# A fused convolution and feed-forward kernel: sums scaled in the first statistics pass, a longer warm-up, a last row cut 320 to 192, and a new order of all instructions

## The chip, the cores and the metric

The kernel runs on one core of a Trainium2 chip. The metric is the time of one execution on the device in microseconds (us); lower is better. A core has five engines that run side by side: TensorE (PE, matmuls and transposes), VectorE (DVE), ScalarE (ACT), GpSimd (POOL) and SyncE (SP), which here only issues transfers. PEld in the profile is TensorE's loading of the stationary operand. Matmuls write to PSUM, eight banks of 128 partitions by 2 KB; everything else lives in SBUF.

## What the reference computes

One sequence of S = 2048 rows with D = 512 columns passes through two pairs of layers, A, B, A, B, all in bfloat16 with the same weights in both pairs.

```
A(q):  k_shift = causal 4-tap convolution of k along the sequence, one set of taps per column
       kv      = k_shift * v
       y       = causal convolution of kv with ssm_k (2048 taps per column, by FFT) + kv * ssm_D
       A(q)    = q * y
B(x):  (silu(x @ w_gate) * (x @ w_up)) @ w_down,   F = 1792

x = A_q
x = x + A(layernorm(x)); x = x + B(layernorm(x))
x = x + A(layernorm(x)); x = x + B(layernorm(x))
```

The layer norm has no weights: (x - mean) / sqrt(var + 1e-5) over the 512 columns. k, v and ssm_k are the same in both A layers, so y is computed once.

## The kernel before

**Tiling.** The sequence is cut into NB = 4 blocks of 512 rows; a block is held as 128 partitions by R = 4 rows. y is made block by block with a short Fourier transform that is a set of matmuls: `fwd` holds cosine and sine tables, `inv` their transposes; H, X and Z are spectra of ssm_k, of kv and of their products. The feed-forward layer takes half a block at a time: a *unit* is (layer, block c, half h) with two rows per partition, and there are 16 of them. For each of 14 tiles `ft` of F a unit makes 4 matmuls of 256 columns for gate and 4 for up (line 968, reported as L311 since the helper `mm` issues them) into a PSUM tile `pf`, ScalarE takes silu of the gate (L970, `sg`) and copies the up part (L974, `ht`), VectorE multiplies them (L977), and the product is the stationary operand of the down matmuls of 512 columns (L990, into `pd`). ScalarE copies `pd` to `dn` (L1034) and VectorE adds it to the block of x, named `xc` (L1037).

**Layer norm.** `prologue` normalises a half block, multiplies it with y, adds it to x, normalises again to `z`, and transposes z into `zT`, the moving operand of gate and up: by transposing transfers on SP (L893), and in the very first unit by TensorE (L920, `ptz`) with one copy each on VectorE and ScalarE (L923, L925). Statistics come from VectorE (`ln_stats`: bnst, mv, ve) or, for eight of the half blocks, from ScalarE (`ln_stats_act`). The latter makes a pass over each of two rows that sums them (L828), one small instruction that multiplies the sums by -1/512 to `nm` (L831), a pass each that squares the row plus nm and sums that (L834), and `ve` (L838). GpSimd raises ve to the power -1/2 (`rstd`).

**Order.** The program does not issue instructions where they are written. Each call of `plan.add` records an instruction with its engine and its buffers; the table `ORDER` gives each of the 1568 its place, and `Plan.issue` emits them by it. Each engine then runs its own instructions in that order and waits by semaphores for the data and the buffers that an instruction needs. Buffers come from rings of a fixed size: `pf` has 4 PSUM tiles, `pc` and `pd` 2 each, `zT` 3, `z` 3, `ht` 5.

**Start.** SP issues the loads of hn (ssm_k of block 0), kn (k), vt (v), xc (q), then those of block 1 and the weight wg, the two table transposes `inv`, and then wu and wd, wd in two parts. VectorE and ScalarE make the tables. TensorE turns the taps (`pt4`, L1133), then transposes hn (16 matmuls, L477) and kn (16, L366). VectorE, ScalarE and GpSimd make 16 diagonal matrices `dg` of the taps (L1152, L1148). Where the planner's own times leave TensorE idle for over 0.5 us before 32 us, `issue` puts in warm-up matmuls `wm` on a constant tile `wz`: their number is the gap, less 0.3 us on both sides at the very start and 0.3 us elsewhere, over 0.106 us.

**End.** The last unit's second row is computed as two halves of 256 columns in two PSUM tiles. x of the second half is added in PSUM by a matmul with the identity (L949). VectorE adds the first half to x (L1008), ScalarE copies the second (L1011), and SP and ScalarE each issue one output transfer (L1014).

Of the kernel before, what the change touches and what calls it, by code (L numbers as in the profile page):

```python
# [9 lines left out]
P = 128  # L10
# [8 lines left out]
NB = 4  # L19
# [31 lines left out]
LASTV = True  # L51
ORDER = [
# [58 lines left out]
]  # L111
R = 4

NS = 8
# [122 lines left out]
def kernel(  # L239
# [984 lines left out]
    def run(unit):  # L1224
        ffn(unit)
# [75 lines left out]
```

## Time and profile before

| | |
|---|---|
| median of 3 runs | 344.79 us (344.21 to 345.18) |
| profiled execution, own time | 344.93 us |
| its span | 343.20 us |
| busy: TensorE, VectorE, ScalarE, GpSimd | 336.4, 283.4, 253.9, 35.3 us |
| first gate matmul, end of the last down matmul | 33.58, 339.98 us |
| waiting transfers at the start: hn of block 0, its issue and first use | 0.72, 4.34 us |

Busy time of TensorE counts every matmul from its start to its modelled end; these overlap, so a busy TensorE may still be far from its full rate. The number behind a line, such as L311, is the line in the kernel, or in the helper that issued the instruction. In a list of events each row has the start, the length, the engine, the line, the tiles written and read, and how many instructions were merged; a bracket gives the engine's idle time just before and what ended it.

### The profile page before, as it was taken

Reading aid. Unit: us, or ns where it says so; the run is one execution under the profiler, and the core shown is the slowest. Engines: PE = TensorE matmul, PEld = TensorE weight load, DVE = VectorE, ACT = ScalarE, POOL = GpSimd, SP = SyncE. Lnnn points to the kernel's source line nnn. Section 1 sums busy time; section 2 is a strip of 40 time slices with the busy share of each in tenths; the row PEclk is TensorE's granted clock in tenths of the full one; section 3 lists DMA queues with packets and bytes.
Section 4 is the critical chain, followed back from the end, with each engine's and each line's share of the span. In section 5 each row is a group of like instructions: output and inputs, shape, how many; then the busy total and the mean of one; then the engine's idle time right before and its main releaser. Section 6 shows DMA issues by size and latency. Waiting matters only on the chain.

```text
span 343.2 us, 6553 instructions
## 1 busy us (share of the span) xinstructions
PE 336.4 (98%) x2579; PEld 248.6 (72%) x2610; DVE 283.4 (83%) x482; ACT 253.9 (74%) x504; POOL 35.3 (10%) x46
## 2 busy tenths in 40 slices
PE   8999999999999999999999999999999999999996
PEld 7756868768687676858586777768685877777783
DVE  8899999899999999899999999989998433726022
ACT  6999999899997765958789995779475464446261
POOL 4010100203111000103110100201101001000000
PEclk9999999999999999999999999999999999999999
DMA  7999218310116044040101014210101100110101
GB/s 273 336 316 341 52 27 112 77 32 0 34 31 94 14 95 138 2 94 3 32 2 46 2 46 79 76 32 1 32 0 33 35 13 0 39 39 8 24 26 37
DMA packets 42088, 22.95 MB, mean 67 GB/s; under 512 B 33861, under 2 KB 39882, under 8 KB 42058
## 3 DMA queue, kind: packets, MB, share of 16 engines
q1 hardware_dynamic: 41904, 22.47, 26.6%
q8 instruction: 20, 0.33, 0.4%
q14 instruction: 10, 0.08, 0.1%
q10 hardware_dynamic: 154, 0.07, 0.1%
HBM read 12.33 MB, written 2.10 MB: 42 GB/s over the span
## 4 chain that ended last, share of the span: by engine, by line
PE 91%; ACT 4%; DVE 3%; issue 1%
PE pf L311 54%; PE pd L990 28%; PE ps L311 6%; PE ps L458 1%; ACT H L419 1%; PE wm L1267 1%; DVE bnst L809 1%; ACT hs L487 1%; PE pt L477 1%; ACT X L419 0%; ACT n L859 0%; PE pt L366 0%; DVE m L540 0%; DVE t L665 0%; DVE Z L667 0%
## 5 line engine op out<-in xcount | busy, mean ns | idle before, releaser
L311 PE MATMUL pf<-zT,wu_sb 128*128 128x256 bf16 x896 | 110.4, 273 | 0.1
L311 PE MATMUL pf<-zT,wg_sb 128*128 128x256 bf16 x896 | 110.2, 273 | 0.2
L990 PE MATMUL pd<-wd_sb,ht 128*128 128x512 bf16 (+1 forms) x440 | 102.4, 372 | 1.2
L311 PEld LDWEIGHTS <-wu_sb 128*128 128x128 bf16 x896 | 87.7, 98 | 16.4
L311 PEld LDWEIGHTS <-wg_sb 128*128 128x128 bf16 x896 | 87.6, 98 | 16.5 <-issue 0.8
L974 ACT CAST ht<-pf 128x512 bf16<-128x512 f32 x112 | 64.0, 591 | 29.3 <-PE pf L311 29.1
L970 ACT ACTIVATE sg<-pf 128x512 bf16<-128x512 f32 x112 | 65.5, 603 | 17.4 <-PE pf L311 15.1
L990 PEld LDWEIGHTS <-ht 128*128 128x128 bf16 x462 | 45.2, 98 | 42.5
L977 DVE TENSOR_TENSOR ht<-ht,sg 128x1024 bf16<-128x1024 bf16 (+1 forms) x64 | 39.0, 617 | 24.0 <-ACT sg L970 18.7
L814 POOL TENSOR_TENSOR rstd<-ve,nhalf 128x2 f32<-128x2 f32 x24 | 23.0, 958 | 217.8 <-DVE ve L812 207.6
L1034 ACT CAST dn<-pd 128x512 bf16<-128x512 f32 x30 | 17.0, 589 | 21.0 <-PE pd L990 20.9
L809 DVE BATCH_NORM_STATS2 bnst<-xc 128x6 f32<-128x512 bf16 x48 | 31.6, 684 | 0.6
L419 ACT ACTIVATE X<-ps 128x512 bf16<-128x512 f32 x32 | 19.2, 611 | 4.0 <-PE ps L311 3.4
L653 DVE TENSOR_TENSOR t<-X,G 128x2048 bf16<-128x2048 bf16 x18 | 21.9, 1218 | 0.1
L657 DVE TENSOR_TENSOR t<-X,G 128x2048 bf16<-128x2048 bf16 x18 | 21.9, 1216 | 0.0
L1037 DVE TENSOR_TENSOR xc<-xc,dn 128x1024 bf16<-128x1024 bf16 x15 | 10.3, 689 | 13.4 <-ACT dn L1034 13.2
L665 DVE TENSOR_TENSOR t<-t,t 128x2048 bf16<-128x2048 bf16 x12 | 14.7, 1222 | 0.3
L667 DVE TENSOR_TENSOR Z<-Z,t 128x2048 bf16<-128x2048 bf16 x12 | 14.6, 1220 | 0.2
L840 POOL TENSOR_TENSOR rstd<-ve,nhalf 128x2 f32<-128x2 f32 x8 | 8.7, 1088 | 59.2 <-ACT ve L838 59.1
L419 ACT ACTIVATE H<-ps 128x512 bf16<-128x512 f32 x24 | 13.8, 610 | 0.1
L886 DVE TENSOR_TENSOR n<-n,Yk 128x1024 bf16<-128x1024 bf16 x15 | 10.3, 688 | 4.1 <-ACT n L859 3.8
L604 ACT ACTIVATE kc<-kTb,tapF 128x512 bf16<-128x512 bf16 x16 | 12.1, 783 | 0.0
(105 smaller groups left out, 323.3 us busy)
## 6 DMA issues: line engine op xcount, KB each, us to landing
hn<-in_A_ssm_k_dram SPq DMA_DIRECT2D x4, 512.0 KB, 4.1
vt<-in_A_v_dram SPq DMA_DIRECT2D x4, 512.0 KB, 5.9
xc<-in_A_q_dram SPq DMA_DIRECT2D x4, 512.0 KB, 5.3
out_dram<-xc SPq DMA_DIRECT2D x15, 128.0 KB, 1.8
wg_sb<-in_B_w_gate_dram SPq DMA_DIRECT2D x1, 1792.0 KB
wu_sb<-in_B_w_up_dram SPq DMA_DIRECT2D x1, 1792.0 KB, 8.5
wd_sb<-in_B_w_down_dram SPq DMA_DIRECT2D x1, 1280.0 KB, 12.0
kn<-in_A_k_dram SPq DMA_DIRECT2D x1, 512.0 KB, 4.5
```

What stands on the lines that cost most here:

```text
L311: nc.tensor.matmul(o, lhsT=lhsT, rhs=rhs, start=(n == 0), stop=(n == len(terms) - 1))
L419: add("ACT", act(D), lambda: nc.scalar.activation(out=view(), in_=ps.t[:], func=ACT.Copy, scale=scale), r=[ps], w=[(buf, keys)], conv=conv)
L653: dve(n * D, lambda t1=t1, part=part: nc.vector.tensor_mul(out=t1.t[:], in0=x.t[:, sl, 0, :], in1=g.t[:, sl, part, :]), [(x, key(slots, (0 ...
L657: dve(n * D, lambda t2=t2, part=part: nc.vector.tensor_mul(out=t2.t[:], in0=x.t[:, sl, 1, :], in1=g.t[:, sl, 1 - part, :]), [(x, key(slots ...
L665: dve(n * D, lambda t1=t1, t2=t2, comb=comb: nc.vector.tensor_tensor(out=t1.t[:], in0=t1.t[:], in1=t2.t[:], op=comb), [t2], [t1], conv=conv)
L809: add("DVE", 0.6, lambda st=st, i=i: nc.vector.bn_stats(out=st.t[:], in_=xs[c].t[:, i, :]), r=[(xs[c], (i,))], w=[st])
L814: add("POOL", pw, lambda: nc.gpsimd.tensor_tensor(out=rstd.t[:], in0=ve.t[:], in1=nhalf.t[:].to_broadcast((P, n)), op=ALU.pow), r=[ve, nha ...
L970: add("ACT", act(D), lambda ps=ps, o=o, sg=sg: nc.scalar.activation(out=sg.t[:, o:o + 2, :], in_=ps.t[:], func=ACT.Silu), r=[ps], w=[(sg, ...
L974: add("ACT", act(D), lambda ps=ps, o=o, ht=ht: nc.scalar.copy(out=ht.t[:, o:o + 2, :], in_=ps.t[:]), r=[ps], w=[(ht, (o // 2,))], due=(uni ...
L977: dve(n * W, lambda sg=sg, ht=ht: nc.vector.tensor_mul(out=ht.t[:], in0=ht.t[:], in1=sg.t[:]), [sg], [ht], due=(unit, k / pairs, 0.0, "h"))
L990: nc.tensor.matmul((pds[o] if not cs.start else pds[HP]).t[:, cs], lhsT=ht.t[:, q, o * P:(o + 1) * P], rhs=wt["d"].t[:, ft, cs], start=(ft ...
L1034: add("ACT", act(D), lambda o=o: nc.scalar.copy(out=dn.t[:, o, :], in_=pds[o].t[:]), r=[pds[o]], w=[(dn, (o,))], due=(unit, 1.0, 3.0, "h"))
```

## The change

- `ln_stats_act` gives its summing pass the scale -1/512, so that the sum is minus the mean, and uses it as nm; the small instruction L831 is gone. The squaring pass of a row depends on that row's sum alone.
- The warm-up's operand is a constant tile of ones that the framework writes, read with step 0; `wz` and its memset are gone. The number of warm-up matmuls leaves out the margins: the gap less 0.3 us at the very start, the whole gap where TensorE falls idle before 8 us, the gap less 0.3 us later.
- The last row is cut into 320 and 192 columns.
- The three `zT` tiles are slices of one tile `zall`.
- The feed-forward code is split into `gate_up` and `down`, which could share a group of tiles between two units. `SHARE` is empty, so each unit makes the same groups of 4, 4, 4 and 2 as before. `VE_D` is off, so `ve` stays on ScalarE.
- The prologue of unit (1, c, 0) is written ahead of unit (0, c, 1); the instructions are the same.
- `ORDER` is a new table with 1559 places, nine fewer: eight times nm and the memset of wz.

In the new order, by comparing the two tables: the transposes of hn run in the order of rows 3, 2, 1, 0 instead of 0, 2, 1, 3 in time, and all 16 transposes of kn come ahead of the first matmul on hs (8 before); VectorE makes six diagonals and two negated tables between tapF and its first copy of hs (four and two before); one matmul group of X1 instead of two, and no statistics pass on ScalarE, precedes the first gate matmul; two evacuations of H come ahead of the first normalisation on ScalarE; on SP the first part of wd is issued behind hn and vt of block 2; on POOL the memset of kTb comes behind three diagonals.

```diff
+TAIL = 320
+VE_D = False
+SHARE = {}
 ORDER = [
-    0, 8, 122, 2, 4, 5, 12, 9, 3, 6, 1, 31, 32, 33, 10, 14, 7, 11, 15, 16, 18, 21, 17, 20, 22, 23, 36, 30, 56, 73, 153, 24, 40, 25, 41, 34, 42, 38,
...
+    0, 14, 2, 4, 6, 8, 21, 1, 3, 5, 12, 13, 63, 9, 10, 11, 7, 16, 22, 19, 17, 18, 20, 23, 30, 43, 31, 73, 88, 89, 29, 44, 25, 36, 26, 45, 24, 33, 55,
...
 ]
+NZ = 3
@@
-                            n = int((start - max(t, 0.3) - 0.3) / 0.106)
+                            n = int((start - t - (0.0 if 0.0 < t < 8.0 else 0.3)) / 0.106)
@@
+        if ring == "zT":
+            def cut(slot):
+                if zall.t is None:
+                    zall.t = zall.make(0)
+                return zall.t[:, slot]
+            return plan.buf(ring, name, cut, parts)
...
+    zall = whole("zT", [P, NZ, KD, HP, P])
@@
-                    out=jk.t[:], in_=xs[c].t[:, i, :], func=ACT.Copy, accum_out=sm.t[:, o:o + 1]), r=[(xs[c], (i,))], w=[jk, (sm, (o,))], after=after)
-        nm = new("mv", "nm", [P, n], F32)
-        add("ACT", TINY, lambda: nc.scalar.mul(out=nm.t[:], in_=sm.t[:, 0:n], mul=-1.0 / D), r=[(sm, range(n))], w=[nm])
+                    out=jk.t[:], in_=xs[c].t[:, i, :], func=ACT.Copy, scale=-1.0 / D, accum_out=sm.t[:, o:o + 1]), r=[(xs[c], (i,))], w=[jk, (sm, (o,))], after=after)
+        nm = sm
...
-                r=[(xs[c], (i,)), nm], w=[jk, (sm, (n + o,))])
+                r=[(xs[c], (i,)), (nm, (o,))], w=[jk, (sm, (n + o,))])
@@
+            halves = (slice(0, TAIL), slice(TAIL, D))
...
-            for half_, (eng, cs) in enumerate((("DVE", slice(0, D // 2)), ("ACT", slice(D // 2, D)))):
+            for half_, (eng, cs) in enumerate((("DVE", slice(0, TAIL)), ("ACT", slice(TAIL, D)))):
@@
-    wz = whole("wz", [P, P])
-    add("DVE", 0.07, lambda: nc.vector.memset(wz.t[:], 0.5), w=[wz], due=-80)
+    ones = nc.const_aps.tensor(1.0, (P, P), BF16)
@@
         run((0, c, 0))
+        prologue(1, c, 0)
         run((0, c, 1))
-        prologue(1, c, 0)
         prologue(1, c, 1)
@@
-            nc.tensor.matmul(t[:], lhsT=wz.t[:], rhs=wz.t[:], start=True, stop=True)
+            nc.tensor.matmul(t[:], lhsT=ones, rhs=ones, start=True, stop=True)
```

More of the change, by code (lines that the diff above doesn't have):

```diff
@@ L231, in issue @@
                 if b.t is None:
-                    b.t = b.make(place.get(b, 0))
+                    b.slot = place.get(b, 0)
+                    b.t = b.make(b.slot)
                 if b in place:
@@ L835, in ln_stats_act @@
                 out=jk.t[:], in_=xs[c].t[:, i, :], func=ACT.Square, bias=nm.t[:, o:o + 1], accum_out=sm.t[:, n + o:n + o + 1]),
-                r=[(xs[c], (i,)), nm], w=[jk, (sm, (n + o,))])
+                r=[(xs[c], (i,)), (nm, (o,))], w=[jk, (sm, (n + o,))])
         ve, rstd = new("ve", "ve", [P, n], F32), new("rs", "rstd", [P, n], F32)
-        add("ACT", TINY, lambda: nc.scalar.activation(out=ve.t[:], in_=sm.t[:, n:2 * n], func=ACT.Identity, scale=1.0 / D, bias=eps.t[:]),
-            r=[(sm, range(n, 2 * n)), eps], w=[ve])
+        if VE_D:
+            add("DVE", 0.08, lambda: nc.vector.tensor_scalar(out=ve.t[:], in0=sm.t[:, n:2 * n], scalar1=1.0 / D, scalar2=LN_EPS,
+                                                             op0=ALU.mult, op1=ALU.add), r=[(sm, range(n, 2 * n))], w=[ve])
+        else:
+            add("ACT", TINY, lambda: nc.scalar.activation(out=ve.t[:], in_=sm.t[:, n:2 * n], func=ACT.Identity, scale=1.0 / D, bias=eps.t[:]),
+                r=[(sm, range(n, 2 * n)), eps], w=[ve])
         add("POOL", PWA, lambda: nc.gpsimd.tensor_tensor(out=rstd.t[:], in0=ve.t[:], in1=nhalf.t[:].to_broadcast((P, n)),
@@ L930, with gate_up, moving, go @@
     LAST_UNIT = (1, NB - 1, HP - 1)
+    UNITS = [(layer, c, h) for c in range(NB) for layer in (0, 1) for h in range(HP)]
+    shared = {}
+    def gate_up(us, fts, k):
+        m, n = len(us), len(fts)
+        per = 2 // m
+        sg = new("sg", "sg", [P, n, m, W], parts=n // per)
+        ht = new("ht", "ht", [P, n, m, W], parts=n // per)
+        zs = [zts[u] for u in us]
+        def moving(kd):
+            if m == 1:
+                return zs[0].t[:, kd]
+            lo, hi = sorted(z.slot for z in zs)
+            return zall.t[:, lo:hi + 1:hi - lo, kd]
+        for b in range(n // per):
+            sl = slice(b * per, b * per + per)
+            for which in ("g", "u"):
+                ps = new("pf", "pf", [P, D], F32)
+                def go(ps=ps, b=b, which=which):
+                    for q in range(per):
+                        ft = fts[b * per + q]
+                        mm(ps.t[:, q * m * W:(q + 1) * m * W],
+                           [(wt[which].t[:, kd, ft * P:(ft + 1) * P], moving(kd)) for kd in range(KD)])
+                at = (k + b * per) / NF
+                add("PE", pe(per * KD, m * W), go, r=[*zs, wt[which]], w=[ps], due=(us[0], at + (which == "u") / 21, 0.0, None))
+                if which == "g":
+                    add("ACT", act(D), lambda ps=ps, sl=sl: nc.scalar.activation(out=sg.t[:, sl], in_=ps.t[:], func=ACT.Silu),
+                        r=[ps], w=[(sg, (b,))], due=(us[0], at, 1.0, "a"))
+                else:
+                    add("ACT", act(D), lambda ps=ps, sl=sl: nc.scalar.copy(out=ht.t[:, sl], in_=ps.t[:]),
+                        r=[ps], w=[(ht, (b,))], due=(us[0], at, 1.5, "a"))
+        dve(n * m * W, lambda: nc.vector.tensor_mul(out=ht.t[:], in0=ht.t[:], in1=sg.t[:]), [sg], [ht], due=(us[0], (k + n) / NF, 0.0, "h"))
+        return ht
@@ new lines, in down, with go @@
+    def down(unit, pds, ht, fts, us, k, first, end, own):
+        for o in range(HP):
+            last = unit == LAST_UNIT and end and o == HP - 1
+            split = unit == LAST_UNIT and o == HP - 1
+            halves = (slice(0, TAIL), slice(TAIL, D))
+            cols = [[cs] for cs in halves] if last else [halves] if split else [[slice(0, D)]]
+            for css in cols:
+                def go(o=o, css=css):
+                    at = sorted(zts[u].slot for u in us).index(zts[unit].slot)
+                    for cs in css:
+                        for q, ft in enumerate(fts):
+                            nc.tensor.matmul((pds[o] if not cs.start else pds[HP]).t[:, cs], lhsT=ht.t[:, q, at, o * P:(o + 1) * P],
+                                             rhs=wt["d"].t[:, ft, cs], start=(first and q == 0 and not own(o, cs)),
+                                             stop=(end and q == len(fts) - 1))
+                n = len(fts)
+                add("PE", pe(n) if not last else pe(n, css[0].stop - css[0].start), go,
+                    r=[ht, (wt["d"], sorted({int(ft >= GROUPS[0]) for ft in fts}))],
+                    w=[pds[o]] if not split else [pds[o], pds[HP]] if not last else [pds[HP if css[0].start else o]],
+                    due=(unit, k / NF, 2.0, None))
@@ L944, in ffn @@
                 i = row(h, o)
-                halves = (slice(0, D // 2), slice(D // 2, D)) if unit == LAST_UNIT and o == HP - 1 else (slice(0, D),)
+                halves = (slice(0, TAIL), slice(TAIL, D)) if unit == LAST_UNIT and o == HP - 1 else (slice(0, D),)
                 halves = [cs for cs in halves if own(o, cs)]
@@ L951, in ffn @@
                     r=[(x, (i,)), ident], w=[pds[HP if cs.start else o] for cs in halves], due=(unit, 2 / pairs, 1.9, None))
-        cuts = [sum(GROUPS[:n]) for n in range(len(GROUPS) + 1)]
-        groups = [range(a, b) for a, b in zip(cuts, cuts[1:])]
-        k = 0
-        for fts in groups:
-            n = len(fts)
-            sg = new("sg", "sg", [P, n, W], parts=n // 2)
-            ht = new("ht", "ht", [P, n, W], parts=n // 2)
-            for o in range(0, n, 2):
-                for which in ("g", "u"):
-                    ps = new("pf", "pf", [P, D], F32)
-                    def go(ps=ps, o=o, which=which, fts=fts):
-                        for q in (0, 1):
-                            ft = fts[o + q]
-                            mm(ps.t[:, q * W:(q + 1) * W],
-                               [(wt[which].t[:, kd, ft * P:(ft + 1) * P], zT.t[:, kd]) for kd in range(KD)])
-                    add("PE", pe(2 * KD, W), go, r=[zT, wt[which]], w=[ps], due=(unit, (k + (which == "u") / 3) / pairs, 0.0, None))
-                    if which == "g":
-                        add("ACT", act(D), lambda ps=ps, o=o, sg=sg: nc.scalar.activation(
-                            out=sg.t[:, o:o + 2, :], in_=ps.t[:], func=ACT.Silu), r=[ps], w=[(sg, (o // 2,))],
-                            due=(unit, k / pairs, 1.0, "a"))
-                    else:
-                        add("ACT", act(D), lambda ps=ps, o=o, ht=ht: nc.scalar.copy(out=ht.t[:, o:o + 2, :], in_=ps.t[:]),
-                            r=[ps], w=[(ht, (o // 2,))], due=(unit, k / pairs, 1.5, "a"))
-                k += 1
-            dve(n * W, lambda sg=sg, ht=ht: nc.vector.tensor_mul(out=ht.t[:], in0=ht.t[:], in1=sg.t[:]), [sg], [ht],
-                due=(unit, k / pairs, 0.0, "h"))
-            for o in range(HP):
-                i = row(h, o)
-                last = unit == LAST_UNIT and fts[-1] == NF - 1 and o == HP - 1
-                split = unit == LAST_UNIT and o == HP - 1
-                halves = (slice(0, D // 2), slice(D // 2, D))
-                cols = [[cs] for cs in halves] if last else [halves] if split else [[slice(0, D)]]
-                for css in cols:
-                    def go(o=o, fts=fts, ht=ht, css=css):
-                        for cs in css:
-                            for q, ft in enumerate(fts):
-                                nc.tensor.matmul((pds[o] if not cs.start else pds[HP]).t[:, cs], lhsT=ht.t[:, q, o * P:(o + 1) * P], rhs=wt["d"].t[:, ft, cs],
-                                                 start=(ft == 0 and not own(o, cs)), stop=(ft == NF - 1))
-                    add("PE", pe(n) if not last else pe(n, D // 2), go, r=[ht, (wt["d"], (0 if fts[0] == 0 else 1,))],
-                        w=[pds[o]] if not split else [pds[o], pds[HP]] if not last else [pds[HP if css[0].start else o]],
-                        due=(unit, k / pairs, 2.0, None))
@@ new lines, in ffn @@
+        left, nxt = shared.pop(unit, []), UNITS[UNITS.index(unit) + 1] if unit != LAST_UNIT else None
+        rest = [ft for ft in range(NF) if all(ft not in fts for _, fts, _ in left)]
+        cut = len(rest) - SHARE.get(unit, 0)
+        groups = left + [(None, rest[a:min(a + 4, cut)], (unit,)) for a in range(0, cut, 4)] \
+            + [(None, rest[a:a + 2], (unit, nxt)) for a in range(cut, len(rest), 2)]
+        k = 0
+        for n, (ht, fts, us) in enumerate(groups):
+            if ht is None:
+                ht = gate_up(us, fts, k)
+                if len(us) > 1:
+                    shared.setdefault(nxt, []).append((ht, fts, us))
+            k += len(fts)
+            down(unit, pds, ht, fts, us, k, n == 0, n == len(groups) - 1, own)
```

6 lines of the change are left out of this document (3 added, 3 removed), and 113 rows, old and new, of the table ORDER.

## The prediction

> **What bounds the kernel now.** I read the page first, then a table of stretches of my own choosing, then the order of events at the start and at the end. From the page:
>
> ```profile
> PE 336.4 (98%) x2579; PEld 248.6 (72%) x2610; DVE 283.4 (83%) x482; ACT 253.9 (74%) x504; POOL 35.3 (10%) x46
> ...
> PE 91%; ACT 4%; DVE 3%; issue 1%
> ```
>
> TensorE is the bound, but a busy share can't tell how tightly its matmuls stand. So I count its work. In the chain 48 matmuls of 256 columns take 5.24 us (109.2 ns each), 12 of 512 take 2.59 us (215.8 ns), 8 transposes take 0.45 us and 16 tap matmuls 0.89 us. With these: 1792 gate and up matmuls 195.7 us, 434 down matmuls of 512 columns and 28 of 256 together 96.7, 136 of the convolution with 512 columns 29.4, 128 tap matmuls 7.1, 56 transposes 3.1: 332 us. The span is 343.2, so 11 us are not work at full rate. The table of stretches says where they lie (columns: length, then busy time of each engine):
>
> ```profile
> 4.34:7.20 2.86, 2.81 (x26) 2.77 (x26) 2.26 (x9) 2.12 (x6) 2.36 (x5) 1.00 0.98 348
> 7.20:14.62 7.42, 7.31 (x88) 5.50 (x88) 6.65 (x13) 6.34 (x16) 0.00 (x0) 1.00 1.03 394
> 14.62:24.50 9.88, 9.44 (x54) 4.74 (x55) 9.47 (x19) 9.12 (x18) 1.04 (x1) 1.00 1.11 275
> 24.50:33.58 9.08, 8.67 (x95) 6.12 (x95) 8.72 (x21) 9.08 (x20) 0.69 (x1) 1.00 1.15 366
> ...
> 100.00:250.00 150.00, 149.32 (x1115) 109.90 (x1125) 145.06 (x215) 114.02 (x228) 15.39 (x14) 1.00 0.22 46
> ...
> 339.98:343.20 3.22, 0.00 (x0) 0.00 (x0) 0.22 (x1) 0.37 (x1) 0.00 (x0) 1.00 0.26 81
> ```
>
> From the first feed-forward matmul (33.58 us) to the last matmul the counted work (195.7 + 96.7 + 62 x 0.2158 for the convolution's rest = 305.9 with the one identity matmul) fills the 306.2 us that it takes. No order can win anything there; it can only lose. What can be won lies before 33.58 and after 339.98. The start, in order of time:
>
> ```profile
> 1.04 2.53 PE L1267 MATMUL wm<-wz 128*128 128x128 bf16 x22 [1.04 <-DVE wz L1050]
> ...
> 3.50 0.29 PE L1133 MATMUL pt<-ident,tapR 4*128 4x4 bf16 x4
> ...
> 3.72 0.71 PE L1267 MATMUL wm<-wz 128*128 128x128 bf16 x5
> ...
> 4.34 1.74 PEld L477 LDWEIGHTS <-hn 128*128 128x128 bf16 x16 [0.18 <-DMA hn<-in_A_ssm_k_dram]
> ...
> 4.49 1.86 PE L477 MATMUL pt<-ident,hn 128*128 128x128 bf16 x16
> ...
> 8.87 0.61 PE L366 MATMUL pt<-ident,kn 128*128 128x128 bf16 x8
> ```
>
> Of the same transposes, 16 take 1.86 us at 4.49 and 8 take 0.61 at 8.87; start to start that is 0.116 against 0.056 us. So TensorE runs at half rate at first, although the granted clock reads 1.00 throughout. The first 512-column matmul starts at 7.00 and its successor 0.36 us later, between the 0.43 of half rate and the 0.216 of full: the rate doubled at about 7.3. The 24 transposes before it lost 24 x 0.056 = 1.3 us. Two idle times follow (the bracket gives the idle time ahead of an instruction and what ended it), and then, below, the end:
>
> ```profile
> 24.51 0.38 PE L311 MATMUL ps<-hs,fwd 128*128 128x512 bf16 x1 [0.40 <-ACT H L419]
> ...
> 31.25 0.39 PE L311 MATMUL ps<-vt,fwd 128*128 128x512 bf16 x1 [0.35 <-DVE vt L515]
> ...
> 33.58 1.04 PE L311 MATMUL pf<-zT,wg_sb 128*128 128x256 bf16 x8
> ```
>
> ```profile
> 339.78 0.42 DVE L1008 TENSOR_TENSOR xc<-xc,pd 128x256 bf16<-128x256 bf16 x1 [0.40 <-PE pd L990]
> 340.00 0.37 ACT L1011 CAST xc<-pd 128x256 bf16<-128x256 f32 x1 [4.12 <-PE pd L990]
> ...
> 340.40 0.38 ACTq L1014 DMA_DIRECT2D out_dram<-xc  x1
> ```
>
> By stream ends, the first is 0.56 us (23.95 to 24.51), the second 0.52 (30.73 to 31.25, behind four warm-up matmuls).
>
> **The change, part by part.** The sum is made against the profiled execution, 344.93 us (span 343.20 and 1.73 around it); the median of the runs shown is 344.79, 0.14 less. 0.3%, about what can be told from no change here, is 1.0 us.
>
> *Warm-up.* The memset of wz (0.17 us on VectorE) goes; the warm-up's operand is a constant that GpSimd has written by 0.4, so TensorE can start where VectorE does, 0.82 instead of 1.04. The first stretch was int((start - 0.6)/0.106) = 22 matmuls, so a start of 2.93 to 3.04, now 24 or 25 of them; the second, 5, becomes 7 or 8. At the measured 0.107 to 0.116 each they fill the pauses at 3.3 to 3.5 and about 4.4. What the rate does has two ends. If it doubles a fixed time after work begins, it did so 7.3 - 1.04 = 6.3 us after, and now does at 7.1: 0.2 us earlier, worth 0.1. If the pauses reset it, it took about 3.6 us from the restart at 3.72 and now comes at about 4.4 to 4.6, and all 1.3 us of the slow transposes could go. But VectorE is late next: after tapF (3.83 to 4.00) the new order has it make six tap diagonals (0.26 each) and two negated tables (0.32) before its first copy of hs: 4.0 + 1.56 + 0.64 = 6.2, ending 6.6, against 5.49 to 5.9 before. The first matmul on hs then starts at 6.65 at the earliest (7.00 before). All 16 transposes of kn come before it now, so 8 of them (0.45 us) no longer lie behind it. Ends: -0.1 and -0.35 - 0.45 = -0.8. I take -0.6, nearer the second: the half rate lasted beyond 6 us only in a stretch with pauses. Against it, three more warm-up matmuls of 0.107 in front of data that lands at 4.30 put the transposes up to 0.3 later; where the rate doubles early this lies under the wait for VectorE, so it is counted only in the other case.
>
> The Trainium skill's page "TensorE: Matmul & The Clock Gate" (Part 1) has the clock released by a free-running window of some 3.4 us of activity; by it the rise falls anywhere from 4.2 to 7.7 in the new kernel, 5.9 on average, and the term would be -0.6 too, differing from execution to execution. Its Part 4 says that transposes do not count as activity and stay slow. By that the new kernel's longer run of transposes would postpone the rise and the term would be zero or a loss. The rows above speak against it: the rate rose after 3 us of almost nothing but transposes, and the eight at 8.87 ran at full rate.
>
> *Statistics.* Eight instructions nm (0.209 us median, and a 0.04 step) leave ScalarE, the other passes keep their 0.64. Before the first feed-forward matmul there is one, at 13.30; ScalarE idles 0.46 us at 14.36 waiting for TensorE, which swallows it: 0, at most -0.24. The other seven lie where TensorE has no idle time: 0.
>
> *Order at the start.* Two evacuations of H now come ahead of the normalisation (0.81 us) that held up the one at 23.86, for which TensorE idled 0.56; the half of it that I take, -0.3, lies between 0 and -0.56 because VectorE, busy without a pause from 16.74 to 27.07, is late next. One 512-column matmul less comes ahead of the first feed-forward matmul (one of X1 instead of two: 0.22), and ScalarE's statistics pass of 0.64 + 0.20, in front of the zT copy at 32.81, moves behind it, with an evacuation of Yk (0.62) in front instead: 0.22 earlier. Both paths agree: -0.2 (0 to -0.4). The 0.52 before 31.25 hangs on the same copy and product as before: 0.
>
> *Queues.* On SP the first part of wd (issued 23.75, landing 10.4 us later) goes behind two 0.5 MB loads (hn and vt of block 2), some 3 us by the 4.1 and 5.9 us these take to land; its first reader is at 44.7, so the cover is 44.7 - 37.2 = 7.5 us: 0. The input loads before it keep their order. On POOL the padding memset of kTb moves behind three diagonals of 0.6 each, to about 6; its reader is at 10.6: 0. The zT tiles become slices of one tile: 0, if waits follow slices.
>
> *Last row.* The final copy has 192 instead of 256 columns: 0.37 x 3/4 plus its fixed part, about 0.31, so the last issue is 0.06 earlier; the identity matmul has 64 columns less, 0.03. On the other side the piece of 320 columns ends two short matmuls (0.17) before the last one instead of 0.22, so VectorE starts 0.05 later and runs about 0.1 longer: SP's issue moves from 340.23 to about 340.38, beside ScalarE's 340.34. Sum -0.1 (0.1 to -0.2).
>
> Sum: -0.6 - 0.3 - 0.2 - 0.1 = -1.2; 344.93 - 1.2 = **343.7**.
>
> **Rivals.**
> 1. The rate rises no earlier: -0.1 + 0.3 for the overfilled warm-up - 0.3 - 0.2 - 0.1 = -0.4, **344.5**, no measurable change. For it: one execution can't show whether the pauses mattered.
> 2. Everything passes through: -0.8 - 0.56 - 0.4 - 0.2 = -2.0, **342.9**. Against it: ScalarE and VectorE are busy 9.1 and 8.7 of the 9.1 us before 33.58.
> 3. Slower: the new order makes TensorE wait for VectorE between 100 and 250 us, where VectorE is busy 145.1 of 150 us. The chain runs from ScalarE at 151.3 through VectorE to a down matmul at 163.34: there is no margin in such places. One product of 2048 columns (1.22 us) put ahead of a product of ht costs up to that; two cost 2.4, and 344.93 - 1.2 + 2.4 = **346.1**. It decides from 2.2 us of waits in sum. Against it: in the present order no such wait reached TensorE at all.
>
> **How the numbers follow.** The forecast's case has 0.44, and its own range is 343.2 to 344.2; three quarters of it (0.33) lie below 343.76, the bound of faster, the rest (0.11) above. Rival 1 has 0.25, rival 2 has 0.12, rival 3 has 0.19. So faster 0.33 + 0.12 = 0.45, same 0.11 + 0.25 = 0.36, slower 0.19. The range 342.6 to 345.7 takes in both unknown ends of the start and leaves out most of rival 3.
>
> **What would show it.** Right: warm-up from 0.82 without a pause, transposes of 0.056 us before 6.5, the first feed-forward matmul near 32.5 and no wait of TensorE above 0.5 us behind it. Wrong: transposes still at 0.11 us up to 7 (rival 1), or rows of TensorE waiting for ht, zT or a transposed tile after 40 us (rival 3).

## The result: 0.7 us slower, and the profile after

The changed kernel takes 345.19 us (median of 22 runs, 344.61 to 346.04), the kernel before, timed beside it, 344.51 (22 runs, 343.95 to 345.18): a ratio of 1.0020, 95% interval 1.0013 to 1.0028. The forecast was a gain of 1.2 us by its sum; the time went the other way by 0.7. Timed again (d1 below) the two had 345.14 against 344.44, 1.0019 (1.0008 to 1.0029).

The profiled execution after takes 344.87 us with a span of 343.1. Its page has, for busy times and for the chain that ended last:

```profile
PE 337.5 (98%) x2615; PEld 247.4 (72%) x2615; DVE 282.7 (82%) x481; ACT 250.8 (73%) x496; POOL 35.0 (10%) x46
...
PE 89%; ACT 6%; DMA 2%; DVE 1%; POOL 1%; issue 0%; SPq 0%
```

TensorE's share of the chain fell from 91% to 89% and VectorE's from 3% to 1%; ScalarE's rose from 4% to 6%, and DMA now has 2%. What TensorE waited for, after (who waits, for what: us in sum, times, longest):

```profile
PE wm L1307 <- PEq L1325: 0.8, 1, 0.8
PE pf L323 <- ACT ht L977: 0.4, 1, 0.4
PE pf L323 <- DMA zT<-z: 0.4, 1, 0.4
PE pt L489 <- DMA hn<-in_A_ssm_k_dram: 0.2, 1, 0.2
PE ps L809 <- DVE m L803: 0.2, 1, 0.2
PE pt L378 <- DMA kn<-in_A_k_dram: 0.2, 1, 0.2
```

The waits for H and for vt near 24 and 31 us (0.40 and 0.35 before) are gone. Five have come: at the start 0.2 each for the loads of hn and kn and for `m`, then 0.4 for `ht` and 0.4 for `zT`, these two in the steady part, where the profile before has none. The start of the same execution, in order of time:

```profile
0.76 2.83 PE L1307 MATMUL wm<-const-bfloat16-1.0 128*128 128x128 bf16 x25 [0.76 <-PEq L1325]
3.52 0.29 PE L1173 MATMUL pt<-ident,tapR 4*128 4x4 bf16 x4
3.74 0.64 PE L1307 MATMUL wm<-const-bfloat16-1.0 128*128 128x128 bf16 x8
4.60 1.08 PE L489 MATMUL pt<-ident,hn 128*128 128x128 bf16 x16 [0.22 <-DMA hn<-in_A_ssm_k_dram]
5.86 1.07 PE L378 MATMUL pt<-ident,kn 128*128 128x128 bf16 x16 [0.17 <-DMA kn<-in_A_k_dram]
...
26.18 0.39 PE L809 MATMUL ps<-m,inv 128*128 128x512 bf16 x1 [0.18 <-DVE m L803]
...
32.43 1.91 PE L323 MATMUL pf<-zT,wg_sb 128*128 128x256 bf16 x16
```

This looks like the forecast: all transposes at 0.056 us, first gate matmul at 32.43 against 33.58, 1.15 us earlier. The eight warm-up matmuls at 3.74 already stand 0.060 us apart, so in this execution the rate had doubled by 3.8. The steady part gives it back. From the first gate matmul to ScalarE's copy of the last row, which I call the *stretch*, it is 33.58 to 340.00 before, 306.42 us, and here 32.43 to 339.82, 307.39: 0.97 more. Of that 0.22 is the X1 matmul of 512 columns that the new order makes behind the first gate matmul instead of ahead of it, and 0.72 the two waits. Here is the first of them in the same list, and what ran ahead of it on ScalarE and GpSimd:

```profile
59.30 1.75 POOL L855 TENSOR_TENSOR rstd<-ve,nhalf 128x2 f32<-128x2 f32 x1 [13.47 <-ACT ve L853]
...
61.08 0.48 ACT L867 ACTIVATE nmr<-sm,rstd 128x1 f32<-128x1 f32 x2 [0.89 <-POOL rstd L855]
61.60 1.52 ACT L874 ACTIVATE n<-xc,nmr,rstd 128x512 bf16<-128x512 bf16 x2
63.02 0.56 ACT L977 CAST ht<-pf 128x512 bf16<-128x512 f32 x1
...
63.64 1.03 PE L323 MATMUL pf<-zT,wg_sb 128*128 128x256 bf16 x8 [0.36 <-ACT ht L977]
```

ScalarE stands idle for 0.89 us until GpSimd has raised two numbers per partition to a power, then makes nmr and two passes n (2.0 us together), and only then the copy `ht` that sets a bank of `pf` free. The kernel before has the same chain at nearly the same place:

```profile
59.97 1.79 POOL L840 TENSOR_TENSOR rstd<-ve,nhalf 128x2 f32<-128x2 f32 x1 [12.88 <-ACT ve L838]
...
61.79 0.48 ACT L852 ACTIVATE nmr<-nm,rstd 128x1 f32<-128x1 f32 x2 [0.86 <-POOL rstd L840]
...
62.18 1.50 ACT L859 ACTIVATE n<-xc,nmr,rstd 128x512 bf16<-128x512 bf16 x2
...
63.59 1.04 ACT L974 CAST ht<-pf 128x512 bf16<-128x512 f32 x2
...
64.20 1.03 PE L311 MATMUL pf<-zT,wg_sb 128*128 128x256 bf16 x8
```

GpSimd is as slow there (1.79 us) and ScalarE idles as long, yet the gate matmul at 64.20 has no idle time ahead of it. So the slow power alone does not make TensorE wait; it depends on what the order leaves TensorE to do meanwhile. The second wait, in the list of events of after:

```profile
222.12 0.72 DVE L879 TENSOR_SCALAR z<-xc,mv,rstd 128x512 bf16<-128x512 bf16 x2
...
227.50 1.05 PE L323 MATMUL pf<-zT,wg_sb 128*128 128x256 bf16 x8 [0.36 <-DMA zT<-z]
```

Here z is ready 1.2 us later than before, counted from the first gate matmul, and its two transposing transfers land 3.6 us after the second is issued, where the median of the kernel's thirty pairs is 2.4. The end:

```profile
339.66 0.49 DVE L1049 TENSOR_TENSOR xc<-xc,pd 128x320 bf16<-128x320 bf16 x1 [1.33 <-PE pd L994]
339.82 0.32 ACT L1052 CAST xc<-pd 128x192 bf16<-128x192 f32 x1 [5.00 <-PE pd L994]
340.18 0.39 ACTq L1055 DMA_DIRECT2D out_dram<-xc  x1
340.18 0.33 SPq L1055 DMA_DIRECT2D out_dram<-xc  x1
```

Copy to issue is 0.36 here and was 0.40. But the two transfers take longer. From issue to landing, before and then after:

```profile
DMA to landing us min/median/max: 1.6/1.6/1.7
...
DMA to landing us min/median/max: 1.8/1.9/1.9
```

ScalarE's transfer, the last to land, takes 1.67 us before and 1.93 after. From the start of ScalarE's copy to the end of the span it is 3.15 us before and 3.27 after.

So by these two profiles the changed kernel should be about even (344.87 against 344.93), while the medians differ by 0.7. The profiles do not show what is usual, and that is the first thing to settle.

### The profile page after: what moved, and what is told of

The parts are those of the page before. It is cut to its first block, busy times and chain, and to the rows that moved or that the text cites. A ratio compares the mean times of both kernels' runs of the same rounds, so it can differ in the third digit from the quotient of the medians.

```text
span 343.1 us, 6584 instructions
## 1 busy us (share of the span) xinstructions
PE 337.5 (98%) x2615; PEld 247.4 (72%) x2615; DVE 282.7 (82%) x481; ACT 250.8 (73%) x496; POOL 35.0 (10%) x46
## 4 chain that ended last, share of the span: by engine, by line
PE 89%; ACT 6%; DMA 2%; DVE 1%; POOL 1%; issue 0%; SPq 0%
PE pf L323 54%; PE pd L994 26%; PE ps L323 6%; PE ps L470 2%; DMA kn<-in_A_k_dram 1%; ACT H L431 1%; DMA zT<-z 1%; ACT n L874 1%; ACT sg L974 1%; ACT ht L977 1%; ACT hr L603 1%; POOL rstd L855 1%; ACT jk L845 0%; ACT jk L840 0%; PE pt L378 0%
## 5 line engine op out<-in xcount | busy, mean ns | idle before, releaser
L323 PE MATMUL pf<-zT,wg_sb 128*128 128x256 bf16 x896 | 110.7, 273 | 0.7 <-ACT ht L977 0.4
L994 PE MATMUL pd<-wd_sb,ht 128*128 128x512 bf16 (+1 forms) x462 | 103.7, 373 | 0.0
L977 ACT CAST ht<-pf 128x512 bf16<-128x512 f32 x112 | 64.2, 594 | 40.1 <-PE pf L323 39.0
L1078 DVE TENSOR_TENSOR xc<-xc,dn 128x1024 bf16<-128x1024 bf16 x15 | 10.3, 685 | 22.9 <-ACT dn L1075 22.9
L901 DVE TENSOR_TENSOR n<-n,Yk 128x1024 bf16<-128x1024 bf16 x15 | 10.3, 689 | 8.6 <-ACT Yk L703 5.2
L616 ACT ACTIVATE ka<-kTb,tapF 128x512 bf16<-128x512 bf16 x16 | 12.4, 788 | 0.0
```

Of the source, the lines that this page charges most:

```text
L323: nc.tensor.matmul(o, lhsT=lhsT, rhs=rhs, start=(n == 0), stop=(n == len(terms) - 1))
L977: add("ACT", act(D), lambda ps=ps, sl=sl: nc.scalar.copy(out=ht.t[:, sl], in_=ps.t[:]), r=[ps], w=[(ht, (b,))], due=(us[0], at, 1.5, "a"))
L994: nc.tensor.matmul((pds[o] if not cs.start else pds[HP]).t[:, cs], lhsT=ht.t[:, q, at, o * P:(o + 1) * P], rhs=wt["d"].t[:, ft, cs], start ...
```

## The experiments

All kernels below compute the whole reference. In all of them the stretch is measured as above, and the time at which TensorE's rate doubled is read from the spacing of its transposes, 0.106 us at half rate and 0.056 at full, and of the matmuls beside them.

**1. All edits but the order (a1, repeated as c3).** The table of the kernel before with the nine places of the removed instructions left out; warm-up, statistics and last row as changed.

```diff
 ORDER = [
-    0, 14, 2, 4, 6, 8, 21, 1, 3, 5, 12, 13, 63, 9,
+    7, 120, 1, 3, 4, 11, 8, 2, 5, 0, 30, 31, 32, 9,
...
 ]
```

> The changed kernel with all 1559 instructions in the order of the kernel before (warm-up, statistics, last row and slices of zT as changed). Theory 1 (the new order pays for waits of TensorE behind 40 us, the small edits do not lose): no such wait, 344.0 to 344.5 us, so at or a little below the kernel before (344.5). Rival (one of the small edits loses, for example the warm-up on a constant read with step 0 or the one tile for zT): 345.2 as the changed kernel, with the loss away from the two waits seen at 63 and 227 us.

Measured: 344.59 us against 344.79 on the same chip, ratio 0.9988 (0.9970 to 1.0005). The stretch is 306.31, without a wait behind 36 us. Again on another chip:

> All edits in the order before, once more, on the same chip as the two others. If the small edits gain in the median what the last row (0.06) and the warm-up bring: 0.1 to 0.3 us below the kernel before, as the first time (0.9988). If they bring nothing: within 0.1 us of it. TensorE's stretch from the first gate matmul to the last copy is 306.3 us, as in its first profile.

Measured: 344.07 against 344.60, 0.9991 (0.9982 to 1.0001), stretch 306.32. The waits of TensorE in this run are those of the kernel before and no others:

```profile
PE wm L1249 <- PEq L1267: 0.8, 1, 0.8
PE ps L265 <- ACT H L373: 0.4, 1, 0.4
PE ps L265 <- DVE vt L469: 0.3, 1, 0.3
```

So the loss needs the new order. The other edits together bring 0.2 to 0.5 us by the medians; both intervals just take in no change. Against the kernel before beside it, this version has the lowest medians that I found.

**2. Halves of the order (a2, a3, b1).** Each table below is spliced from the two, with all other edits as changed: a2 the new order up to the first gate matmul and the old one behind it; a3 the old one up to there and the new one behind it; b1 the new one up to the third group of gate and up, then the old one, with two X1 groups made later.

```diff
 ORDER = [
-    0, 14, 2, 4, 6, 8, 21, 1, 3, 5, 12, 13, 63, 9,
+    7, 120, 1, 3, 4, 11, 8, 2, 5, 0, 30, 31, 32, 9,
...
 ]
```

(That is a3; a2 and b1 begin as the new table does and differ from it behind the splice.)

> The changed kernel, in the new order up to the first gate matmul (without its one X1 group) and in the order before from there. Theory 1: the start keeps what it gained in the profile (first gate matmul near 32.2) and TensorE does not wait later: 343.2 to 343.7 us, below both kernels. Rival a (the early start only moves TensorE into waits for z that is made no sooner): 344.3 to 344.8, with a wait for zT or ht between 40 and 230. Rival b (a small edit loses): above 345.

> The changed kernel, in the order before up to the first gate matmul (without its two X1 groups) and in the new order from there. Theory 1 (the waits belong to the new order of the rest): 345.5 to 346.2 us, waits at the same places. Rival a (the waits come only since the first gate matmul is 1.1 us earlier): 344.2 to 344.7 and no wait above 0.3 us.

> Again the new order for the start and the order before for the rest, but cut behind the third gate or up group, and with the two X1 groups that made TensorE wait 0.7 us at the first cut moved behind the groups that follow. Theory 2 (the new start is worth something in a usual execution, and only the new order of the rest gives it back): 343.6 to 344.1 us, first gate matmul near 32.4, no wait above 0.3 us behind 40. Rival (z of the next units is made no sooner, so an early start ends in a wait for zT): 344.4 to 345.0 with such a wait between 40 and 100 us.

Measured: a2 345.74 (1.0023, 1.0010 to 1.0036), a3 347.33 (1.0065, 1.0043 to 1.0087), b1 348.02 (1.0093, 1.0079 to 1.0107). a3 and b1 are slower than either whole order and a2 is about as slow as the new one, because the splice itself costs: in a2 the first matmuls of X1 wait 0.69 us for ScalarE's X just ahead of the first gate matmul, in a3 a copy `ht` is stuck behind a slow rstd. From the list of events of a3:

```profile
38.50 2.53 POOL L797 TENSOR_TENSOR rstd<-ve,nhalf 128x2 f32<-128x2 f32 x1 [7.55 <-ACT ve L795]
41.07 0.48 ACT L809 ACTIVATE nmr<-sm,rstd 128x1 f32<-128x1 f32 x2 [1.20 <-POOL rstd L797]
...
43.48 1.03 PE L265 MATMUL pf<-zT,wu_sb 128*128 128x256 bf16 x8 [1.75 <-ACT ht L919]
```

These three don't say which half of the order costs the 0.7. What a3 shows is the mechanism of the wait at 63.6, five times as long: GpSimd's power, then n on ScalarE, then the copy for which TensorE waits.

**3. The warm-up's old count (a4).** The kernel after with the pauses of before: 22 and 5 matmuls, on the new constant.

```diff
-                            n = int((start - t - (0.0 if 0.0 < t < 8.0 else 0.3)) / 0.106)
+                            n = int((start - max(t, 0.3) - 0.3) / 0.106)
```

> The changed kernel with the number of warm-up matmuls as before (22 and 5 instead of 25 and 8, still on the constant). If the pauses held the rate of TensorE down until 7.3 us in the profile before: the transposes of hn run at 0.11 us each again, the first gate matmul 0.4 to 0.7 later, 345.5 to 345.9 us. If the moment at which the rate rises does not depend on the pauses: 345.0 to 345.3, as the changed kernel.

Measured: 345.98 (344.30 to 347.13), ratio 1.0023 (1.0003 to 1.0043), the widest spread of all; the kernel before beside it spreads from 344.17 to 346.79. The profiled execution took 346.80, near the upper end. Its start:

```profile
3.42 0.72 PE L1307 MATMUL wm<-const-bfloat16-1.0 128*128 128x128 bf16 x5
4.80 1.90 PE L489 MATMUL pt<-ident,hn 128*128 128x128 bf16 x16 [0.66 <-DMA hn<-in_A_ssm_k_dram]
6.49 1.91 PE L378 MATMUL pt<-ident,kn 128*128 128x128 bf16 x16
```

All 32 transposes are at half rate, the rate doubles only at about 10.3, and the first gate matmul comes at 34.90, 2.5 us later than in the profile of after. The new order has all of kn's transposes ahead of the first matmul on hs, and in this one execution it paid for a late rate.

**4. The copy ahead of n (b2).** In the new order the `ht` that TensorE waits for at 63.6 goes ahead of the two n, with its gate matmuls.

```diff
-    375, 374,
+    376, 375,
...
-    377,
+    374,
...
-    376,
+    377,
```

> The changed kernel with one ScalarE instruction moved: the copy ht that TensorE waits for at 63.6 us comes ahead of the two normalisations (0.7 us each) that stand before it. If that wait costs its 0.4 to 0.6 us at the end: the wait is gone and the time is 344.6 to 344.9. If the time is given back at the next unit, because z comes 0.6 later: 345.1 to 345.4 and a wait for zT behind 70 us.

Measured: 345.73 (345.07 to 346.79), ratio 1.0028 (1.0015 to 1.0041), stretch 308.58. The wait for ht is gone, and others have come. From the waits of TensorE:

```profile
PE pf L265 <- DMA zT<-z: 1.1, 2, 0.7
...
PE pf L265 <- ACT sg L916: 0.3, 1, 0.3
```

With n later, VectorE's product with it comes 0.34 us later, counted from the first gate matmul. The two waits for zT stand at 110.7 and 229.1, far behind; how they come from the move was not followed. So one instruction moved took one wait away and brought others, longer in sum.

**5. Both kernels profiled again (b3 before, b4 after).** No edit.

> The kernel before once more, for a second profile of its start. If the rate of TensorE always rises near 7.3 us with the pauses in the warm-up: 16 transposes of hn in 1.8 to 1.9 us and the first gate matmul near 33.6 again. If the moment varies freely: somewhere between 4.4 and 7.9, and the first gate matmul between 32.9 and 33.7.

> The changed kernel once more. If the warm-up without pauses makes the rate rise before the transposes each time: 16 of hn in 1.1 us and the first gate matmul near 32.4 again. If it varies freely, a rise between 4.2 and 7.7 us, with the first gate matmul up to 1.3 us later when late; the two waits near 63 and 227 us again in either case if they belong to the order.

Measured, one execution each: 344.62 and 345.38. The start of b3, the kernel before:

```profile
4.76 1.29 PE L477 MATMUL pt<-ident,hn 128*128 128x128 bf16 x16 [0.31 <-DMA hn<-in_A_ssm_k_dram]
6.02 0.62 PE L366 MATMUL pt<-ident,kn 128*128 128x128 bf16 x8
...
32.91 1.04 PE L311 MATMUL pf<-zT,wg_sb 128*128 128x256 bf16 x8
```

Its first five transposes are 0.1 us apart and the others 0.056, so the rate doubles at about 5.3, not 7.3, with the same warm-up and the same pauses; and the first gate matmul stands at 32.91, 0.67 earlier than in the profile from which I forecast. This execution lies on the median of the runs beside it. b4 has its first gate matmul at 32.97, since both loads landed late, hn at 5.07 (TensorE waited 0.73 for it) and kn at 6.35. It has the same two waits as after, at 64.2 and 228.0, 0.36 and 0.32 long: they are no accident of one execution.

**6. Only the overfill undone (c1, c2, d1, d2).** 25 matmuls in the first stretch as changed, but 5 in the second instead of 8; in c1 with the old order, in c2 and d2 with the new one. d1 is the kernel after itself.

```diff
-                            n = int((start - t - (0.0 if 0.0 < t < 8.0 else 0.3)) / 0.106)
+                            n = int((start - t - 0.3) / 0.106)
```

> All edits, the order before, and a second warm-up stretch of 5 matmuls instead of 8 (the first stays 25). In four of the profiles with 8 the transposes of hn begin at 4.83 us, where the eighth one ends, and with 5 they began at 4.49 to 4.8, with the data. If the three matmuls too many cost what they push back: 0.1 to 0.3 us below the same kernel with 8, 344.2 to 344.4, and the best of all. If the pause makes the rate rise later instead: the same or above, 344.6 to 345.0, with a rise behind 6 us.

> The changed kernel in its new order with 25 and 5 warm-up matmuls. If only the matmuls too many count: 345.0 to 345.2. If the new order needs the rate up early, since all 24 remaining transposes and 16 of kn come ahead of its first matmul on hs, and the pause delays it: 345.5 to 346.2.

Measured on one chip: c1 344.38, 1.0000 (0.9989 to 1.0012); c2 344.40, 0.9996 (0.9986 to 1.0006). So the new order with three matmuls less was no slower than the kernel before, which I had not expected by so much. Since the kernel after was not timed on that chip, both went to one chip:

> The kernel after the change, unedited, timed on the same chip as the 25-and-5 version below. If the three extra warm-up matmuls cost something of their own (hn's transposes at 4.83 in place of 4.51): 0.3 us above d2, and the stretch from the first gate matmul to the last row's copy still 306.9 or more. If only the two small waits of the new order set its time: 344.9 to 345.4, ratio 1.001 to 1.003, and d2 the same within 0.2. If neither, so that the earlier pair of medians (345.19 and 344.40) was two chips: both at 344.4 to 344.8 here.

> The kernel after with warm-ups of 25 and 5. Three extra matmuls cost of their own: 0.3 us below d1, ratio near 1.000. Only the waits: the same as d1 within 0.2, at 344.9 to 345.4, with one or both of the waits for ht (63.6) and zT (about 228) in its profile and a stretch of 306.9 to 307.4.

Measured: d1 345.14, 1.0019 (1.0008 to 1.0029); d2 344.59, 1.0004 (0.9992 to 1.0017). By the runs the difference of the medians is 0.56 us (0.24 to 1.04, by resampling the two sets of 12). So by the medians, taking the three matmuls out brings back most of the loss in the new order. Start and first gate matmul of d1, with the loading of kn's transposes, and from its page the us from kn's issue to its landing:

```profile
3.74 1.03 PE L1307 MATMUL wm<-const-bfloat16-1.0 128*128 128x128 bf16 x8
4.83 1.86 PE L489 MATMUL pt<-ident,hn 128*128 128x128 bf16 x16
6.80 0.90 PEld L378 LDWEIGHTS <-kn 128*128 128x128 bf16 x16 [0.37 <-DMA kn<-in_A_k_dram]
6.80 1.07 PE L378 MATMUL pt<-ident,kn 128*128 128x128 bf16 x16
...
33.37 1.91 PE L323 MATMUL pf<-zT,wg_sb 128*128 128x256 bf16 x16
...
kn<-in_A_k_dram SPq DMA_DIRECT2D x1, 512.0 KB, 5.5
```

and of d2:

```profile
3.74 0.71 PE L1307 MATMUL wm<-const-bfloat16-1.0 128*128 128x128 bf16 x5
4.51 1.86 PE L489 MATMUL pt<-ident,hn 128*128 128x128 bf16 x16
6.17 1.14 PE L378 MATMUL pt<-ident,kn 128*128 128x128 bf16 x16
...
32.81 1.91 PE L323 MATMUL pf<-zT,wg_sb 128*128 128x256 bf16 x16
...
kn<-in_A_k_dram SPq DMA_DIRECT2D x1, 512.0 KB, 4.3
```

Neither waits for hn: the data is there, and its transposes start when the warm-up ends, at 4.83 or 4.51. But in this pair of profiles that 0.32 is not what moved the first gate matmul by 0.56. Both have the same issue of kn at 1.24; it landed at 6.75 in d1 and at 5.51 in d2. In d1 kn's transposes start 0.05 behind that landing, 0.3 after hn's could have ended, and they would have started no sooner with hn's at 4.51. The rate doubled at about the same time, between 6.4 and 6.8 in d1 and at 6.4 in d2. So the medians show that the new order is faster without the three matmuls, and this pair does not show by what. Where the rate is late and kn lands early, the 0.32 would count in full; that is an estimate from the two starts.

The stretch is 307.01 and 306.87, and this difference is in the transfers near 223. The second of the pair is issued 191.4 us behind the first gate matmul in all six profiles of the new order in the table below, but the pair lands 3.6, 3.6 and 3.2 us later with 8 matmuls (after, b4, d1) and 2.5 with 5 (c2, d2, a4). The wait for zT comes only with the former (in d1 it leaves 0.14 us of stretch and no row of its own). Why they land later I can't say, and three against three don't show that the matmuls have to do with it: every profile, those of before too, has a pair somewhere that takes 3.2 us or more.

In the old order the same three matmuls did not cost anything: c1, without them, has a median 0.31 above c3 on the same chip (-0.08 to 0.69). In c1's profile kn's transposes waited 0.35 us for kn's data, so an earlier end of hn's gained nothing; whether that is the whole reason stays open.

The profiles side by side (us; start of hn's transposes, doubling of the rate, landing of kn, start of kn's transposes, first gate matmul, stretch, waits behind 36 us):

```
                        hn     rate    kn in   kn     gate   stretch  waits
before                 4.49     7.3    5.71   6.15   33.58   306.42   none
before again (b3)      4.76     5.3    5.97   6.02   32.91   306.73   zT 0.2
old order (a1)         4.83     5.8    5.74   6.15   33.04   306.31   none
old order (c3)         4.83     5.5    5.62   6.02   32.91   306.32   none
old order, 25+5 (c1)   4.51     4.6    5.89   5.93   32.84   306.33   none
after                  4.60    <3.8    5.81   5.86   32.43   307.39   ht 0.36, zT 0.36
after again (b4)       5.12    <3.8    6.35   6.39   32.97   307.36   ht 0.36, zT 0.32
after again (d1)       4.83   6.4-6.8  6.75   6.80   33.37   307.01   ht 0.36
after, 25+5 (c2)       4.51     5.4    5.52   5.79   32.36   306.87   ht 0.37
after, 25+5 (d2)       4.51     6.4    5.51   6.17   32.81   306.87   ht 0.36
after, 22+5 (a4)       4.80    10.3    6.03   6.49   34.90   306.86   ht 0.36
```

The start of kn's transposes fixes the first gate matmul. From the one to the other it is 26.9 us in the four profiles of the old order below the first row and 26.6 in the five of the new order above the last; only before (27.4) and a4 (28.4), where the rate doubled over 1 us behind that start, need more. And kn's transposes start either 0.05 us behind kn's landing or when hn's are done.

## Why the prediction was wrong, step by step

**The warm-up, -0.6: mis-sized, and the first step that failed.** The reading that the pauses held the rate down until 7.3 rested on one execution. With the same pauses b3 doubled at 5.3, and with the pauses filled the rate doubled anywhere from below 3.8 (after, b4) to 6.8 (b1). The working also took VectorE as the next that is late, with its first copy of hs at 6.2. It was ready: in the profile of after that copy starts at 5.75. What TensorE waits for in all three profiles of the kernel after is a load that the working left out: kn, which landed at 5.81, 6.35 and 6.75 (5.71 and 5.97 in the two profiles of before, the first of which has no wait for it). A longer warm-up moves no load. The three have their first gate matmul at 32.92 on average, b3 at 32.91: nothing is left of the gain there. The 1.15 us between the first two profiles was in good part luck: the one from which I forecast lost 0.54 us behind the start of kn's transposes that b3 did not lose, and the first profile of after has the earliest kn of its three.

A later rate in kernels with pauses is not ruled out (7.3, 5.3 and 10.3 with 22 and 5 matmuls, against below 3.8 to 6.8 with 25 and 8), but what it was worth is bounded by the runs with the old order: 0.2 to 0.5 us by the medians for all edits but the order, where the working had 0.7 for warm-up and last row. A smaller slip: the half-rate transposes stand 0.107 apart, not 0.116, so the 24 of them lost 1.2 us and not 1.3.

The Trainium skill's page "TensorE: Matmul & The Clock Gate" (Part 1) has a window of 3.4 us that runs freely, and says that the same kernel shows other numbers of cold matmuls (those at half rate) from run to run. The spread above agrees in kind; it is wider than the 0.5 us to both sides that the page names. I quoted that rule and still took the size from one profile, and the two rises before 3.8 lie outside my estimate of 4.2 to 7.7 from it. Its Part 4, that transposes stay slow, is contradicted once more: in b4 the sixteen of hn ran at 0.056 us from the first one. Whether they count as activity as other matmuls do stays open: in a4 the rate did not rise in 3.4 us of unbroken transposes, only 2.1 us behind the first matmul on hs.

**The overfill, "up to 0.3 later": the push is there, its price is open.** The working counted it only where the rate rises late, on the ground that otherwise it lies under the wait for VectorE. With 8 matmuls at half rate the transposes start at 4.83 in all six runs whose data was there (a1, a3, b1, b2, c3, d1), with 5 at 4.51. By the medians of d1 and d2 the three matmuls cost 0.56 us (0.24 to 1.04) in the new order, and in the old order nothing; in the one pair of profiles kn's landing hides what the push did.

**Order at the start, -0.3 for the evacuations of H: the wait went, the gain did not come.** From the first transpose of kn to the first gate matmul it is 26.89 us in b3 and 26.57 in the profile of after; 0.22 of the difference is the X1 matmul, so 0.10 is left. The working named who is late next, VectorE, and that is what the profile shows at 26.18: the matmul starts 0.35 us after its predecessor could have ended, waiting for m.

**One X1 group fewer, -0.2: counted once, but it has two ends.** The matmul comes out of the start, where the first gate matmul gains 0.22, and goes into a stretch of which the same text says that it has no room; there it costs 0.22. The step should have been 0. This one needed no chip to find.

**From 33.58 on, 0: wrong by 0.4 to 0.7.** The counted bound was right, since no run has a stretch below 306.3. "It can only lose" was right as well, and rival 3 had the kind of loss, but the forecast took none. The waits are 0.36 or 0.37 for ht in all six profiles of the new order in the table and 0 to 0.36 for zT. Rival 3 looked to VectorE and to places between 100 and 250 us and priced a product of 1.22; the wait that always comes is on ScalarE at 63.6, behind GpSimd. Of the signs that the text named for being wrong, the first nearly came (d1 still has transposes 0.107 apart at 6.3) and the second did: every profile of the new order in the table has a row that waits for ht behind 40 us. That no wait reached TensorE in the order of before was no evidence for another order, and a change of all places needed a term of its own there.

**Statistics, 0.** Nothing in the runs speaks against it: ScalarE's busy time fell from 253.9 to 250.8 and the stretches with the old order, 306.31 to 306.33, are 0.1 from the 306.42 of before, though eight small instructions are gone.

**Queues, 0.** No wait on wd or kTb appears in the waits of after.

**Last row, -0.1: it came out at +0.1.** The copy takes 0.32 instead of 0.37, and SP and ScalarE issue together at 340.18, 0.36 behind the copy's start instead of 0.40, as worked out. But the working ended at the issue. From the start of the copy to the end of the span it is 3.25 to 3.28 us in all nine profiles of the table with the new cut, and 3.15 and 3.17 in the two of before, since the last transfer lands 1.93 us behind its issue instead of 1.67. No run tells whether that is the common moment of the two issues or the new sizes; ScalarE's piece is the smaller one now and lands later all the same.

The balance against the repeated profile of before: start 0.0, stretch +0.5 (mean of the three profiles of after, 307.25, less 306.73), end +0.1: +0.6 of the 0.7 that the medians show. Against the mean of both profiles of before (33.25 and 306.58) it would be start -0.3, stretch +0.7 and end +0.1. So the loss behind the start is seen in every profile of the kernel after, and how much of it an earlier start gives back hangs on the executions that happened to be profiled.

## What to carry to other kernels

Before a start-up term is costed, profile the unchanged kernel twice, and read the landing of every load in it: here one execution had the rate double 2.0 us later than the next, and the forecast's largest term, 0.6 us, rested on that one. When work is moved out of a stretch, book it where it goes to, and at full price if that stretch is full. Follow the end to the landing of the last transfer and not only to its issue. In this kernel, whose bound engine has no idle time behind the start, a new order had nothing to gain there and found waits of 0.4 to 0.7 us. A warm-up that runs past the landing of the first data can push the work behind it (4.51 to 4.83 here).

## What I had not expected of the hardware

- The rate of TensorE doubled before 3.8 us in two executions of one kernel and between 6.4 and 6.8 in a third, with the same warm-up, and at 10.3 in a kernel whose warm-up had pauses; the granted clock read 1.00 throughout, so only the spacing of matmuls shows it.
- Loads issued at the same time land at different times: hn between 4.22 and 5.07 us and kn between 5.48 and 6.75 in the fifteen profiles, both issued before 1.3.
- Two output transfers issued at one moment landed 1.76 and 1.93 us later, where 0.17 us apart they had taken 1.58 and 1.67. Their sizes had changed as well.
- GpSimd's power of two numbers per partition takes from 0.69 to 1.75 us within one kernel, 2.53 in a3, and ScalarE's n waits for it. In the profile of after, all seven that run while VectorE is idle take 0.69, and all seven above 1.2 us have more than 1 us of VectorE's two-operand products beside them. No run separates the two.
- Pairs of transposing transfers that land after 2.4 us in the median took 3.2 to 3.6 at the same place in three profiles and 2.5 in three, with the same issue relative to TensorE.
